# A 768 KB weight load cut into ten transfers of 64 to 3 rows, in a decode kernel with a full DMA queue

## The chip, the cores and the metric

The kernel runs on one core of one Trainium2 chip. A core has a matrix engine (PE, with PEld for its weight loads), a vector engine (DVE), a scalar engine (ACT), a general one (POOL), a queue engine (SP), and 16 DMA engines that move data between the chip's memory and the core's own memory of 128 partitions. The metric is device time in microseconds of one execution, the median over several runs. Before the change it is 1329.57 us (three runs, 1329.53 to 1329.71).

## The reference

Two blocks read the same input `x` (2 batches, 1 position, 1024 wide) and are mixed by a gate. Cut to what matters:

```python
def _A_ref(x, k_cache, v_cache, wq, wo):          # 32 heads, 16384 cached positions, 128 wide
    q = (x @ wq).reshape(B, Sq, H, Dh).transpose(0, 2, 1, 3)
    scores = jnp.einsum("bhqd,bhkd->bhqk", q, k_cache) * (Dh ** -0.5)
    p = _softmax(scores, axis=-1)
    o = jnp.einsum("bhqk,bhkd->bhqd", p, v_cache)
    return o.transpose(0, 2, 1, 3).reshape(B, Sq, H * Dh) @ wo

def _B_ref(x, w1, w2, w3, w4):
    h = _gelu(_layernorm(x) @ w1)
    ...                                            # four quarters of h shifted by 1, -1, 2, -2 positions
    x1 = x + hs @ w2
    return x1 + _gelu(_layernorm(x1) @ w3) @ w4

g = _sigmoid((x * gate_w).sum(-1, keepdims=True))
return g * a + (1 - g) * b
```

Everything is bfloat16. The two caches are 2 x 32 x 16384 x 128 each, 268 MB each, and are read once. With one position per batch, every shift moves `h` out of the sequence, so `hs` is zero; the kernel still computes `h`.

## The kernel before

All bulk data goes through one on-chip array, `mem`, of 128 partitions and five cells of 32 KB per partition. A K or V load is two heads of one batch: 8 MB, 64 KB in each partition, two cells. K of batch 0 lies in cells 0 and 1, K of batch 1 in cells 1 and 2, V in cells 3 and 4. There are 32 such units (16 head pairs by 2 batches), each with a K load (`load_k`, line 113) and a V load (`load_v`, line 118). All of them are issued by SP, in the order of the program, each as soon as the cells that it fills have been read.

For a unit, DVE transposes K in blocks (line 435), PE forms the scores (line 441), ACT the exponentials (line 479), and PE the product with V (line 495). A loop (line 684) runs over the head pairs; the last unit stands apart and issues the tail loads (`load_tail`, line 567): wo, w4 in three pieces, and the last five row groups of w1 in three pieces, each with a semaphore of its own on which PE waits. When the last piece of w1 has landed, PE adds its product (line 402), ACT applies the gelu (line 663) and the program ends; the output has been stored meanwhile (line 586).

Ahead of all this stands the start. A weight matrix of 1024 rows is laid out with eight row groups in each partition. SP issues, in this order: the first three row groups of w1 (`w1_early`, line 98: 128 partitions of 6 KB, into cell 1), the two rows of x (line 101), the row of the gate weights (line 102), and wq, 8 MB (line 91, into cells 3 and 4). ACT issues w2, 2 MB, on its own queue. PE turns x (line 235), DVE, PE and POOL compute the layer norm (`layernorm_T`), and PE multiplies the result by the three early row groups (`rows4`, line 207); ACT saves the sum in `h_early` (line 327), from which the tail goes on. Then come w2's products and wq's. The first K load goes into cells 0 and 1, over `w1_early`, and so waits on SP until PE has read it; w3 waits for wq's cells, and so on.

`in_order` (line 668) fixes the order of the instructions on each engine as the program has them.

Of the kernel before, what the change touches and what calls it, by code (L numbers as in the profile page):

```python
# [23 lines left out]
def kernel(  # L24
# [15 lines left out]
    nc = tc.nc  # L40
    P = nc.NUM_PARTITIONS
    B, Sq, D = A_x.shape
# [4 lines left out]
    KC = D // P  # L47
    FC = F // P
# [10 lines left out]
    Q4 = 4  # L59
    QP = P // Q4  # L60
    CELL = NJ * Dh // 2
    G1 = D // Q4
# [17 lines left out]
    def region(cell, elements, offset=0):  # L80
        at = cell * CELL + offset
        return mem[:, at : at + elements]

    def load_weight(W, cell, offset=0, pieces=None, queue=nc.sync):
        K, N = W.shape
        dst = region(cell, K // P * N, offset)
        src = W.rearrange("(p r) n -> p (r n)", p=P)
        r = 0
        for n in pieces or (K // P,):
            at = slice(r * N, (r + n) * N)  # L90
            queue.dma_start(out=dst[:, at], in_=src[:, at])
            r += n
        return dst.rearrange("p (r n) -> p r n", n=N)

    W1_EARLY = 3
    w1_rows = B_w1.rearrange("(p r) n -> p (r n)", p=P)
    w1_early = region(1, W1_EARLY * D)
    nc.sync.dma_start(out=w1_early, in_=w1_rows[:, 0 : W1_EARLY * D])
    w2 = load_weight(B_w2, 2, queue=nc.scalar)
    rows = const.tile([B + 1, D], BF16, name="rows")  # L100
    nc.sync.dma_start(out=rows[0:B], in_=A_x.rearrange("b s n -> (b s) n"))
    nc.sync.dma_start(out=rows[B : B + 1], in_=gate_w.unsqueeze(0))
    wq = load_weight(A_wq, 3)

    K_CELL = (0, 1)
# [11 lines left out]
    def load_v(hp, b, cell=V_CELL):  # L117
# [7 lines left out]
        out=ident_s[:], in0=ident_f[:], scalar1=-scale, scalar2=None, op0=ALU.mult  # L125
# [10 lines left out]
        out=mask4[:], in_=mask4[:], compare_op=ALU.is_ge, fill=0.0,  # L136
# [3 lines left out]
        out=mask4[:], in_=mask4[:], compare_op=ALU.is_ge, fill=0.0,  # L140
# [11 lines left out]
        out=lmat[:].rearrange("p (g h k) -> p g h k", h=2, k=4),  # L152
        in_=hm2[:].unsqueeze(1).unsqueeze(3).to_broadcast([P, P // 8, 2, 4]),
# [5 lines left out]
        out=lane[:],  # L159
        in_=ident_f[:].rearrange("p (c k) -> p k c", k=QP),  # L160
# [5 lines left out]
    for g in range(Q4):  # L166
        nc.vector.tensor_scalar(
            out=spread[:, g],
# [4 lines left out]
    oacc = [ops.tile([P, 4 * Dh], FP32, name=f"oacc{k}") for k in range(2)]  # L173
# [3 lines left out]
    arows = [ops.tile([P, G1], FP32, name=f"arow{k}") for k in range(2)]  # L177
# [18 lines left out]
    def rows4(acc, actT, weight, R, at, n, G, added=None):  # L196
        for g in range(Q4 if added is not None else 0):
            nc.tensor.matmul(
                acc[QP * g : QP * g + B, 0:n],
                lhsT=ident_b[0:B, 0:B],  # L200
                rhs=added[:, g * G + at : g * G + at + n],
                start=True,
                stop=False,
            )
        for r in range(R):
            for g in range(Q4):
                nc.tensor.matmul(
                    acc[QP * g : QP * g + B, 0:n],
                    lhsT=actT[:, r, :],
                    rhs=weight[:, r, g * G + at : g * G + at + n],  # L210
                    start=(r == 0 and added is None),
                    stop=(r == R - 1),
                )

    def turned(wide, C):
        t = mlp.tile([P, C, QP], FP32, tag="turn", name="turn")
        nc.vector.transpose(  # L217
            out=t[:].rearrange("p c k -> p (c k)"), in_=wide.rearrange("p c k -> p (c k)")
        )
        return t[:, :, 0:B]  # L220
# [13 lines left out]
    for r in range(KC):  # L234
        nc.tensor.matmul(
            rows_ps[:, r], lhsT=rows[:].rearrange("b (p r) -> b r p", r=KC)[:, r],
            rhs=ident_b[:], start=True, stop=True,
# [73 lines left out]
    xn1T = mlp.tile([P, KC, B], BF16)  # L311
    shT = mlp.tile([P, KC, B], BF16)
    xn2T = mlp.tile([P, KC, B], BF16)
    h2T = mlp.tile([P, FC, B], BF16)

    def spread_batch(t, C):
# [3 lines left out]
    compute_gate()  # L320
    layernorm_T(xT, xn1T[:], "ln1")
    nc.vector.memset(shT[:], 0.0)
    rows4(
        oacc[0], xn1T, w1_early.rearrange("p (r n) -> p r n", n=D), W1_EARLY, 0, G1, G1
    )
    h_early = const.tile([P, G1], FP32, name="h_early")
    nc.scalar.activation(out=h_early[:], in_=oacc[0][:, 0:G1], func=ACTF.Copy)
    for shift in (1, -1, 2, -2):
# [10 lines left out]
        out=x1_rows[:], in_=oacc[1][:, 0:G1], func=ACTF.Copy, scale=omg_row[:, 0:1]  # L339
# [21 lines left out]
    for k in range(2):  # L361
        wide = mlp.tile([P, 16, QP], FP32, tag="wide", name="wide")
        nc.scalar.activation(  # L363
            out=wide[:].rearrange("p (c e) i -> p c e i", e=2),
            in_=oacc[k][:].rearrange("p (c i e) -> p c e i", i=QP, e=2),
# [6 lines left out]
    for g in range(Q4):  # L372
        nc.tensor.matmul(
            qdps[:, :, :, g, :],
            lhsT=spread[:, g].rearrange("p a k -> p (a k)"),
            rhs=qb[:].rearrange("p a k x b v -> p a k (x b v)"),
            start=True,
            stop=True,
        )
    qdu = const.tile([P, NU, NV], BF16, name="qdu")  # L380
    for e in range(2):
        half = slice(e * HALF, (e + 1) * HALF)
        nc.vector.tensor_copy(
            out=qdu[half].rearrange("p u v -> p (u v)"),
            in_=qdps[half, e].rearrange("p k g n -> p (k g n)"),
# [8 lines left out]
            op=ALU.mult,  # L394
        )


    def add_rows(into, actT, first, weight, last, group):
        n = weight.shape[1] // D
        for r in range(n):  # L400
            for g in range(Q4):
                mm = nc.tensor.matmul(  # L402
                    into[g][QP * g : QP * g + B, 0:G1],
                    lhsT=actT[:, first + r, :],
                    rhs=weight[:, r * D + g * G1 : r * D + (g + 1) * G1],
                    start=False,
                    stop=(last and r == n - 1),
                    skip_group_check=True,
                )
                tc.declare_no_dep(mm.ins, group=group, reason="tail semaphores")  # L410
        return mm

    def begin_rows(into, saved):
        for g in range(Q4):
            nc.tensor.matmul(
                into[g][QP * g : QP * g + B, 0:G1],
                lhsT=ident_f[:, QP * g : QP * g + B],
                rhs=saved[:],
                start=True,
                stop=False,  # L420
                skip_group_check=True,
            )
# [103 lines left out]
    def turn_heads():  # L526
        apart = mlp.tile([P, B, H, Q4], BF16, name="apart")
        for b in range(B):
            nc.vector.tensor_tensor(
                out=apart[:, b],  # L530
                in0=o_all[:, b].unsqueeze(2).to_broadcast([P, H, Q4]),
                in1=mask4[:].unsqueeze(1).to_broadcast([P, H, Q4]),
                op=ALU.mult,
            )
        ps = misc_psum([P, B, QP])
        for b in range(B):
            nc.tensor.matmul(
                ps[:, b], lhsT=apart[:, b].rearrange("p h c -> p (h c)"), rhs=lane_b[:],
                start=True, stop=True,
            )  # L540
        t = mlp.tile([P, QP, B], BF16, name="o_turned")
        nc.vector.tensor_copy(out=t[:], in_=ps[:].rearrange("p b r -> p r b"))
        return t
# [17 lines left out]
    def tail_piece(k):  # L561
        group, cell, at, src, r, n = TAIL[k]
        return region(cell, n * D, at * D)
# [14 lines left out]
    def write_out():  # L578
        for g in range(Q4):
            at = out_row[:, g * G1 : (g + 1) * G1]  # L580
            row = arows[g][QP * g : QP * g + B, :]
            if g % 2 == 0:
                nc.vector.tensor_copy(out=at, in_=row)  # L583
            else:
                nc.scalar.activation(out=at, in_=row, func=ACTF.Copy)
        dma = nc.scalar.dma_start(out=out.rearrange("b s n -> (b s) n"), in_=out_row[:])
        dma.then_inc(stored, 16)
        tc.no_tile_sem_insts.add(dma.ins.name)
        tc.add_to_no_dep_group("stored", dma.ins)
# [53 lines left out]
    def output():  # L643
        begin_rows(arows, x1_rows)
        o_turned = turn_heads()
        hidden = [oacc[0]] * Q4
        begin_rows(hidden, h_early)
        nc.scalar.activation(
            out=h_rows[0:1, 0:1], in_=o_turned[0:1, 0, 0:1], func=ACTF.Gelu_apprx_tanh
        )  # L650
        for k, (group, cell, at, src, r, n) in enumerate(TAIL):
            nc.tensor.wait_ge(tail_sems[k], 16)
            if src is wo_rows:
                add_rows(arows, o_turned, 0, tail_piece(k), False, group)
            elif src is w4_rows:
                mm = add_rows(arows, h2T, r, tail_piece(k), r + n == FC, group)
                if r + n == FC:
                    tc.declare_fence(mm.ins, group=group)
                    write_out()
            else:  # L660
                mm = add_rows(hidden, xn1T, r, tail_piece(k), r + n == KC, group)
                tc.declare_fence(mm.ins, group=group)
        nc.scalar.activation(out=h_rows[:], in_=oacc[0][:, 0:G1], func=ACTF.Gelu_apprx_tanh)  # L663
        mark = nc.gpsimd.memset(end_mark[:], 0.0)
        tc.declare_fence(mark.ins, group="stored")
        nc.gpsimd.wait_ge(stored, 16)
# [62 lines left out]
```

## Time and profile before

| what | before |
|---|---|
| median of three runs | 1329.57 us |
| the profiled execution: time, span | 1329.7 us, 1327.7 us |
| PE busy, share of the span | 760.3 us, 57% |
| DVE busy | 647.6 us, 49% |
| ACT busy | 132.5 us, 10% |
| DMA: bytes, mean rate | 572.69 MB, 431 GB/s |
| `w1_early`: issue to landing | 8.8 us |

The profile shows one execution. The span runs from the first to the last instruction on the core; the execution's own time is longer by what lies around it. The page cuts the span into 40 slices, with a digit for the busy tenths of each engine, and for the DMA engines the mean share of the 16 and the rate. The DMA queue that SP issues to is q1, that of ACT is q10; q8 and q14 bring instructions. A transfer counts its completion on a semaphore, one step for each DMA engine that took part; the trace holds the time of each step, and start, length and size of every DMA packet.

### The profile page before, as it was taken

To read this page: it belongs to the slowest core of one execution; us is meant where nothing else is said; L and a number is where in the kernel's file an instruction comes from. 1 tells how busy PE (TensorE), PEld (TensorE's weight loads), DVE (VectorE), ACT (ScalarE), POOL (GpSimd) and SP (SyncE) were. 2 spreads that over 40 slices of the span, in tenths; PEclk is the share of its full clock that TensorE was granted. 3 is DMA by queue.
4 is the path that set the end of the run, shared out by engine and by line. 5 is a ranking of instruction groups with operands and counts; after the bars stand their busy time and mean duration, and the time that the engine had idled before them with its cause. 6 is when DMAs were issued, how large, how long until landed. Compare 5 with 4: busy or idle time off the path is not lost.

```text
span 1327.7 us, 12974 instructions
## 1 busy us (share of the span) xinstructions
PE 760.3 (57%) x4956; PEld 330.6 (25%) x4956; DVE 647.6 (49%) x507; ACT 132.5 (10%) x207; POOL 12.1 (1%) x48
## 2 busy tenths in 40 slices
PE   3465566655556665555666555566655556665554
PEld 1122222222222222222222222222222223222222
DVE  2554455554445555444555544455554445555420
ACT  0011110011111001111100111110011111101110
POOL 1000000000000000000000000000000000000000
PEclk9677888777788877778887777888777788877776
DMA  9999999999999999999999999999999999999998
GB/s 403 441 439 423 435 434 438 424 432 440 438 426 432 440 423 434 438 440 424 432 440 434 428 434 438 424 434 438 440 424 432 440 424 432 438 440 424 432 440 369
DMA packets 10820, 572.69 MB, mean 431 GB/s; under 512 B 1205, under 2 KB 1205, under 8 KB 1850
## 3 DMA queue, kind: packets, MB, share of 16 engines
q1 hardware_dynamic: 10662, 570.44, 99.4%
q10 hardware_dynamic: 148, 2.10, 0.4%
q8 instruction: 8, 0.13, 0.0%
q14 instruction: 2, 0.02, 0.0%
HBM read 572.53 MB, written 0.00 MB: 431 GB/s over the span
## 4 chain that ended last, share of the span: by engine, by line
DMA 61%; PE 11%; DVE 10%; issue 4%; ACT 0%; DVEq 0%; PEld 0%; SPq 0%; ACTq 0%
DMA mem<-in_A_k_cache_dram 59%; PE S L441 11%; DVE KT L435 10%; DMA mem<-in_B_w_dram 3%; PE oacc L495 0%; DVEq L435 0%; ACT pt L479 0%; PEld L495 0%; SPq L113 0%; PE misc L513 0%; PE oacc L402 0%; ACT osb L508 0%; PEld misc L488 0%; ACT h_rows L663 0%; PE misc L472 0%
## 5 line engine op out<-in xcount | busy, mean ns | idle before, releaser
L441 PE MATMUL S<-KT,qw 128*128 128x512 bf16 x2048 | 548.2, 418 | 363.2 <-DVE KT L435 362.8
L435 DVE STREAM_TRANSPOSE KT<-mem 128x2048 f32<-128x2048 f32 x256 | 570.7, 2282 | 270.9 <-DMA mem<-in_A_k_cache_dram 212.0
L441 PEld LDWEIGHTS <-qw 128*128 128x128 bf16 x2048 | 216.5, 106 | 686.8 <-issue 482.6
L495 PE MATMUL oacc<-mem,pt 128*8 128x512 bf16 x2048 | 118.2, 384 | 7.6 <-DMA mem<-in_A_v_cache_dram 7.6
L466 ACT ACTIVATE Dm<-ident_s,m 128x128 f32<-128x128 f32 x32 | 12.9, 402 | 978.5 <-PE oacc L495 941.4
L479 ACT ACTIVATE pt<-St,nb 64x256 bf16<-64x256 f32 x64 | 89.7, 1401 | 61.1 <-DVE nb L477 60.2
L517 DVE TENSOR_SCALAR o_all<-misc,g_rep 128x2 f32 (+1 forms) x32 | 7.0, 220 | 163.2 <-PE misc L513 163.2
L488 PE MATMUL misc<-rs,lmat 128*128 128x1 f32 x64 | 18.7, 362 | 107.9 <-ACT pt L479 61.3
L495 PEld LDWEIGHTS <-pt 128*8 128x8 bf16 x2048 | 47.3, 87 | 75.6 <-issue 23.8
L513 PE MATMUL misc<-lane,osb 128*128 128x2 f32 x256 | 33.4, 252 | 45.3 <-ACT osb L508 45.3
L489 DVE RECIPROCAL rinv<-misc 128x1 f32<-128x1 f32 x32 | 5.4, 169 | 108.5 <-PE misc L488 60.5
L462 DVE STREAM_TRANSPOSE St<-S 128x512 f32<-128x512 f32 x32 | 22.9, 717 | 66.4 <-PE L495 64.4
L513 PEld LDWEIGHTS misc<-lane,osb 128*128 128x128 f32 x256 | 31.1, 191 | 61.0 <-ACT osb L508 31.6
L488 PEld LDWEIGHTS misc<-rs,lmat 128*128 128x128 f32 x64 | 16.0, 311 | 114.8 <-ACT pt L479 65.3
L508 ACT ACTIVATE osb<-oacc,rinv 128x512 f32<-128x512 f32 x32 | 22.0, 687 | 88.3 <-PE oacc L495 88.3
L479 ACT ACTIVATION_READ_ACCUMULATOR pt<-St,nb 64x1 f32 x64 | 30.6, 477 | 0.0
L389 POOL TENSOR_TENSOR qw<-qdu,mask 128x16 bf16<-128x16 bf16 x32 | 7.3, 261 | 1161.6 <-PEq L688 1074.6
L477 DVE TENSOR_REDUCE nb<-misc 64x1 f32<-64x64 f32 x64 | 14.2, 222 | 7.0 <-PE misc L472 4.9
L472 PE MATMUL misc<-Dm,ones_f 128*128 128x128 f32 x64 | 16.6, 346 | 0.0
L464 DVE TENSOR_REDUCE m<-St 128x1 f32<-128x256 f32 x32 | 13.4, 420 | 1.1
L583 DVE CAST out_row<-arow 2x256 bf16<-2x256 f32 x1 | 0.4, 413 | 26.9 <-PE S L402 26.9
L217 DVE STREAM_TRANSPOSE turn<-wide 128x512 f32<-128x512 f32 (+2 forms) x4 | 3.0, 744 | 17.5 <-ACT wide L363 11.5
(104 smaller groups left out, 95.4 us busy)
## 6 DMA issues: line engine op xcount, KB each, us to landing
mem<-in_B_w_dram SPq DMA_DIRECT2D x1, 7168.0 KB, 31.6
mem<-in_B_w_dram SPq DMA_DIRECT2D x1, 4096.0 KB, 42.1
mem<-in_B_w_dram SPq DMA_DIRECT2D x1, 2304.0 KB, 32.2
mem<-in_B_w_dram ACTq DMA_DIRECT2D x1, 2048.0 KB, 11.8
mem<-in_B_w_dram SPq DMA_DIRECT2D x2, 768.0 KB, 21.1
mem<-in_B_w_dram SPq DMA_DIRECT2D x2, 512.0 KB, 33.9
mem<-in_A_k_cache_dram SPq DMA_DIRECT2D x32, 27.8
mem<-in_A_v_cache_dram SPq DMA_DIRECT2D x32, 32.4
```

The costliest lines, as they stand in the source:

```text
L435: nc.vector.transpose(out=kt[:], in_=Kc.rearrange("p j d -> p (j d)").bitcast(FP32))
L441: nc.tensor.matmul(S, lhsT=qw[b][:, v, NG - 1 - m : NG - 1 - m + P], rhs=ktb[:, half * GT : (half + 1) * GT, w, :, e], start=(first and n ...
L462: nc.vector.transpose(out=st[:].rearrange("p j r -> p (j r)"), in_=S[:])
L464: nc.vector.tensor_reduce(out=m[:], in_=st[:, :, 0:NG], axis=AX.XY, op=ALU.max)
L466: nc.scalar.activation(out=Dm[:], in_=ident_s[:], func=ACTF.Copy, scale=m[:, 0:1])
L472: nc.tensor.matmul(R_ps[:], lhsT=ones_f[:], rhs=Dm[:], start=True, stop=True)
L477: nc.vector.tensor_reduce(out=nb[rows], in_=R_ps[rows, rows], axis=AX.X, op=ALU.min)
L479: nc.scalar.activation(out=pts[b][rows, :, e, :].rearrange("p (m a) k -> p a k m", a=GT // 4), in_=st[rows, :, 0:NG].rearrange("p (a k) m ...
L488: nc.tensor.matmul(tot_ps[:], lhsT=lmat[:], rhs=rs[:], start=True, stop=True)
L495: nc.tensor.matmul(oacc[b][QP * q : QP * q + 8, :], lhsT=pts[b][:, g].rearrange("p h k -> p (h k)"), rhs=V[:, 4 * g : 4 * g + 4, :].rearra ...
L508: nc.scalar.activation(out=osb[:], in_=oacc[b][:], func=ACTF.Copy, scale=rinvs[b][:, 0:1])
L513: nc.tensor.matmul(ot[:], lhsT=osb[:, k * Dh : (k + 1) * Dh], rhs=lane[:, k : k + 5 : 4], start=(k == 0), stop=(k == 3),)
```

## The change

The load of `w1_early` becomes ten transfers: the first 64 partitions in the old place, ahead of x and the gate weights, and 16, 16, 10, 5, 5, 3, 3, 3 and 3 partitions behind these two and ahead of wq. All ten go through SP and count on one semaphore of their own, `early`, taken out of the framework's own bookkeeping. PE waits for all ten (160 steps) ahead of the first matmul that reads them. The matmuls are the same twelve, now recorded by `add_rows`, which moves up in the file and takes a `begin` argument.

```diff
-    nc.sync.dma_start(out=w1_early, in_=w1_rows[:, 0 : W1_EARLY * D])
+    EARLY_ROWS = (64, 16, 16, 10, 5, 5, 3, 3, 3, 3)
+    assert sum(EARLY_ROWS) == P
+    early_sem = tc.alloc_semaphore("early")
+
+    def load_early(pieces):
+        for end, n in pieces:
+            at = slice(end - n, end)
+            dma = nc.sync.dma_start(out=w1_early[at], in_=w1_rows[at, 0 : W1_EARLY * D])
+            dma.then_inc(early_sem, 16)
+            tc.no_tile_sem_insts.add(dma.ins.name)
+            tc.add_to_no_dep_group("early", dma.ins)
+
+    early_pieces = [(P - sum(EARLY_ROWS[:k]), n) for k, n in enumerate(EARLY_ROWS)]
+    load_early(early_pieces[:1])
     w2 = load_weight(B_w2, 2, queue=nc.scalar)
     rows = const.tile([B + 1, D], BF16, name="rows")
     nc.sync.dma_start(out=rows[0:B], in_=A_x.rearrange("b s n -> (b s) n"))
     nc.sync.dma_start(out=rows[B : B + 1], in_=gate_w.unsqueeze(0))
+    load_early(early_pieces[1:])
     wq = load_weight(A_wq, 3)
...
-    rows4(
-        oacc[0], xn1T, w1_early.rearrange("p (r n) -> p r n", n=D), W1_EARLY, 0, G1, G1
-    )
+    nc.tensor.wait_ge(early_sem, 16 * len(EARLY_ROWS))
+    mm = add_rows([oacc[0]] * Q4, xn1T, 0, w1_early, True, True, "early")
+    tc.declare_fence(mm.ins, group="early")
...
-    def add_rows(into, actT, first, weight, last, group):
+    def add_rows(into, actT, first, weight, begin, last, group):
...
-                    start=False,
+                    start=(begin and r == 0),
```

The slices are taken from the end: the 64 rows are partitions 64 to 127, and the last piece is partitions 0 to 2.

More of the change, by code (lines that the diff above doesn't have):

```diff
@@ L213, in rows4 @@
                 )
+    def add_rows(into, actT, first, weight, begin, last, group):
+        n = weight.shape[1] // D
+        for r in range(n):
+            for g in range(Q4):
+                mm = nc.tensor.matmul(
+                    into[g][QP * g : QP * g + B, 0:G1],
+                    lhsT=actT[:, first + r, :],
+                    rhs=weight[:, r * D + g * G1 : r * D + (g + 1) * G1],
+                    start=(begin and r == 0),
+                    stop=(last and r == n - 1),
+                    skip_group_check=True,
+                )
+                tc.declare_no_dep(mm.ins, group=group, reason="tail semaphores")
+        return mm
     def turned(wide, C):
@@ L395, in write_qw @@
         )
-    def add_rows(into, actT, first, weight, last, group):
[L399 to L405, printed above, removed]
-                    start=False,
[L407 to L411, printed above, removed]
     def begin_rows(into, saved):
@@ L653, in output @@
             if src is wo_rows:
-                add_rows(arows, o_turned, 0, tail_piece(k), False, group)
+                add_rows(arows, o_turned, 0, tail_piece(k), False, False, group)
             elif src is w4_rows:
-                mm = add_rows(arows, h2T, r, tail_piece(k), r + n == FC, group)
+                mm = add_rows(arows, h2T, r, tail_piece(k), False, r + n == FC, group)
                 if r + n == FC:
@@ L660, in output @@
             else:
-                mm = add_rows(hidden, xn1T, r, tail_piece(k), r + n == KC, group)
+                mm = add_rows(hidden, xn1T, r, tail_piece(k), False, r + n == KC, group)
                 tc.declare_fence(mm.ins, group=group)
```

## The prediction

> **What bounds the kernel now.** I read the page's slices and queues first, then the timeline of the start and the end, the windows of the end, and last the packet records of the trace.
>
> The page: slices of the DMA share, of the rate, and the queues.
> ```profile
> DMA  9999999999999999999999999999999999999998
> GB/s 403 441 439 423 435 434 438 424 432 440 438 426 432 440 423 434 438 440 424 432 440 434 428 434 438 424 434 438 440 424 432 440 424 432 438 440 424 432 440 369
> ...
> q1 hardware_dynamic: 10662, 570.44, 99.4%
> q10 hardware_dynamic: 148, 2.10, 0.4%
> q8 instruction: 8, 0.13, 0.0%
> q14 instruction: 2, 0.02, 0.0%
> ```
> The 16 DMA engines are busy from end to end, while PE, the busiest compute engine, has 57%. So only three things can move the end: more bytes (there are none: 128 rows of 6 KB before and after), a hole in the stream, or another split of the bytes over the 16 engines.
>
> Holes: the timeline of the start (start, length, engine, line).
> ```profile
> 0.80 0.38 SPq L98 DMA_DIRECT2D mem<-in_B_w_dram  x1
> 0.80 0.42 ACTq L91 DMA_DIRECT2D mem<-in_B_w_dram  x1
> ...
> 1.25 0.33 SPq L101 DMA_DIRECT2D rows<-in_A_x_dram  x1
> ...
> 1.63 0.22 SPq L102 DMA_DIRECT2D rows<-in_gate_w_dram  x1
> ...
> 1.89 0.36 SPq L91 DMA_DIRECT2D mem<-in_A_wq_dram  x1
> ...
> 17.32 0.35 SPq L113 DMA_DIRECT2D mem<-in_A_k_cache_dram  x1
> ```
> The load that waits for the changed matmuls is the first K load at 17.32. The transfer ahead of it, wq, lands its first sixteenth at 29.08 (semaphore events of the trace), so K is queued 11.8 us early. For every later load that lead is 3.7 us or more.
>
> Split: windows of the end (length; PE, PEld, DVE, ACT, POOL busy; clock; DMA share; GB/s), and the chain that ended last.
> ```profile
> 1320.00:1323.00 3.00, 1.71 (x40) 1.00 (x44) 0.00 (x0) 0.00 (x0) 0.00 (x0) 0.76 0.98 391
> 1323.00:1324.00 1.00, 0.73 (x12) 0.16 (x12) 0.24 (x1) 0.20 (x1) 0.00 (x0) 0.50 0.97 379
> 1324.00:1325.00 1.00, 0.60 (x8) 0.10 (x8) 0.59 (x2) 0.55 (x2) 0.00 (x0) 0.50 0.59 234
> 1325.00:1326.00 1.00, 0.57 (x8) 0.10 (x8) 0.00 (x0) 0.00 (x0) 0.00 (x0) 0.50 0.21 80
> ```
> ```profile
> 1291.11 34.28 DMA mem<-in_B_w_dram
> 1325.39 0.04 issue
> 1325.43 0.60 PE oacc L402 x8
> 1326.03 0.03 issue
> 1326.06 0.41 PE oacc L402 x3
> 1326.47 0.02 issue
> 1326.49 0.38 ACT h_rows L663
> ```
> The share falls 0.97, 0.59, 0.21: the engines run dry at different times, and the end hangs on the last of them. The last w1 transfer's sixteen completions come at 1324.23 plus 0, .06, .10, .23, .26, .51, .75, 1.05, 1.46, 1.50, 1.55, 1.62, 1.69, 1.70, 1.71 and 1.79 us, their mean 1.00.
>
> Where the 1.79 us come from: strung together by their times (a packet starts 3 or 4 ns before the last one on its engine ends), the packets give sixteen chains, each with 528 packets of 64 KB and under 0.2 us idle in all. So each engine is a queue that is never empty, and what it gets extra stays to the end. The eight 16 KB packets of q8 each hold one chain up for about 1.55 us, and the two 8 KB ones of q14 one each for about 0.9 and 0.7; no chain gets two of q8. Those are the eight late engines, and those at 1.05 and .75. The views do not number engines.
>
> **The change, part by part.**
> *Rows by engine.* The x transfer (2 rows) shows two packets, on two chains, and gate (1 row) one packet on one of the same two; so a small transfer uses as many engines as it has rows, beginning with the same ones. Then 64 rows are 4 on each engine, 16 are 1, and 10, 5 and 3 are 1 on the first 10, 5 and 3. In place of 8 rows each, engines 0 to 2 get 4+1+1+1+1+1+4 = 13, 3 and 4 get 9, 5 to 9 get 7, and 10 to 15 get 6. A row is 0.231 us (a 6 KB packet takes 234 ns and the next starts 3 ns before its end). A piece ends on each of its engines in a 4-byte packet of 9 ns, 6 net; they have 10, 6, 4 and 3 of these for 1 before. So engines 0 to 2 get 5 x 0.231 + 9 x 0.006 = +1.21 us, 3 and 4 +0.26, 5 to 9 -0.21, and 10 to 15 -0.45.
>
> [...]
>
> *What the end gains.* The first packets started in two groups, eight chains from 1.834 to 1.941 us and eight from 2.037 to 2.371; the x and gate chains (1.834 and 1.891) are in the first. Of the five q8 packets before 162 us, three can be put on a chain for certain, all in the second group; the other two tie with one. I take the second group for engines 8 to 15 and the late eight. Then the last of them moves from 1.79 to 1.34 (if it is among 10 to 15) or 1.58 (if it is 8 or 9), and engines 0 to 2, if they are of the five earliest, to 1.21 to 1.47. The new last is at 1.34 to 1.58, which is 0.21 to 0.45 us earlier. I take -0.30, about the middle.
>
> *Issue on SP.* Nine more issues stand ahead of wq. SP's rows take 0.22 to 0.38 us and stand 0.26 to 0.45 apart, so wq goes from 1.89 to between 4.2 and 5.9. From issue to first packet it was 1.03 us (0.80 to 1.834). Wq's first packets were at 9.19 to 9.80 on the sixteen chains; engines 10 to 15 will want theirs 0.45 earlier, the first at 8.7, so wq must be issued by 7.7. At 5.9 there are 1.8 us left: nothing. From below there is no gain either, as no chain has a hole. A piece that took as long as the 1.03 us to a first packet would cost: wq issued at 11.2, first packets at 12.2, and 3.5 us idle.
>
> *Order on the queue.* x comes behind 4 w1 rows in place of 8, each alternating with a 0.61 us w2 row, so about 4 x 0.84 = 3.4 us sooner; the layer norm from 10.36 to 16.46 moves with it, to about 13. The last rows of engines 0 to 2 end by about 10.2 (1.83 + 13 x 0.23 + 8 x 0.61 + some 0.5 of slow first packets), before that. K's first load then goes out near 14 in place of 17.32, into a queue that is full until 29: 0. If the pieces were late instead, PE would hold there with w2's and wq's matmuls queued behind it, and SP with the K load; 11.8 us cover that.
>
> *PE.* The same 12 matmuls (16.46 to 17.27), now behind a wait for ten transfers, all landed by then: 0. *End.* The store (issued 1324.71, landed 1325.96) follows the w4 piece that landed at 1322.88, which has the same spread (1.86) and moves with it.
>
> Sum: the profiled execution is 1329.70 (span 1327.7 and 2.0 around it), 0.13 over the median of 1329.57. 1329.70 - 0.30 = 1329.40, against the median 1329.27; I say 1329.3.
>
> **The rivals.**
> - *One of engines 0 to 2 is a middling one* (.51, .75 or 1.05, the last two held up by a q14 packet): it ends at 1.72, 1.96 or 2.26, that is -0.07, +0.17 or +0.47, up to 1330.0. For it: the packet at 67.5 us hit one of two or three chains tied in time, one of them x's. Chance 0.28.
> - *One of engines 0 to 2 is a late one*: 1.46 to 1.79 + 1.21, which is +0.88 to +1.21, 1330.5 to 1330.8. For it: gate's chain ties with the one that the packet at 111 us hit. Against it: the two groups. Chance 0.14.
> - *The small transfers cost issue or a fixed time* (slower): from 0.65 us a piece, (7.7 - 1.89) / 9, wq comes too late for the engines; from 0.95 us that is over 2.7 us, and at 1.03 us 3.5 us, 1333.1. Against it: w1, x and gate are followed by the next issue after 0.45, 0.38 and 0.26, and on the chains x, its completion, gate and wq follow each other without a hole. Chance 0.04.
> - *The rows are spread evenly after all* (all pieces on 16 engines by bytes): 0, 1329.6. Against it: x's two packets. Chance 0.03.
>
> [...]
>
> **How the numbers follow.** My forecast, 1329.3, has 0.50 (the -0.21 to -0.45 gives 1329.1 to 1329.4); the remaining 0.01 is for what I have not thought of. Levelling wholly would bring 1.79 - 1.00 = 0.8 us, so faster by 0.2% (2.66 us, about what a measurement here can tell) is out of reach: 0.005. Slower by that needs the issue rival: 0.04. Range: down to 1328.9 (-0.45 and some 0.2 between executions, as the median's runs span 1329.53 to 1329.71), up to 1330.4, which holds the middling and the even case and leaves out the late and the issue one.
>
> **What would show it.** Right: wq issued near 5 us and no hole before its packets; the first K load issued several us before 17; landings of K's first load still near 50.3; three chains with 13 w1 rows; the last w1 completions closer together than 1.79 us, the last by 0.2 to 0.45 sooner. Wrong: a spread of over 2 us with one or a few stragglers (the first two rivals), or a DMA share below 9 tenths near 8 us (the third).

## The result and the profile after

The change made the kernel slower: 1333.11 us (median of 10 runs, 1332.61 to 1334.01) against 1329.66 (10 runs of the kernel before on the same chip, 1329.53 to 1329.92). That is +3.45 us, a ratio of 1.0027 with a 95% interval of 1.0017 to 1.0036. The prediction was 1329.3, with 1328.9 to 1330.4 as its range. The profiled execution is the longest of the ten (1334.01, span 1331.5), so its span grew by 3.8 us, a little more than the median.

The page after: slices of the DMA share and of the rate, and the queues.
```profile
DMA  9999999999999999999999999999999999999998
GB/s 364 435 428 434 430 435 437 431 429 437 435 431 429 437 437 429 431 435 437 433 433 431 437 431 435 429 437 435 433 429 435 437 431 429 437 435 431 431 435 374
...
q1 hardware_dynamic: 10726, 570.44, 99.2%
q10 hardware_dynamic: 148, 2.10, 0.5%
q8 instruction: 8, 0.13, 0.0%
```
Queues and bytes are the same, with 64 more packets on q1, and the busy share is as full as before, from end to end. What differs is the first slice of the rate: 364 GB/s where it was 403. A slice is 33.3 us, so the engines moved 39 x 33.3 us = 1.3 MB less in it, which at the 434 GB/s of a typical slice is 3.0 us. (The page counts a packet whole in the slice in which it starts, and these are packets of 64 KB, so the figure is coarse.) No later slice pays it back. Busy engines that move less: the packets took longer.

The timeline of the start (start, length, engine, line; in brackets the idle time before and what ended it).
```profile
0.81 0.56 SPq L105 DMA_DIRECT2D mem<-in_B_w_dram  x1
...
1.43 0.47 SPq L114 DMA_DIRECT2D rows<-in_A_x_dram  x1
1.96 0.23 SPq L115 DMA_DIRECT2D rows<-in_gate_w_dram  x1
2.23 3.29 SPq L105 DMA_DIRECT2D mem<-in_B_w_dram  x9
5.56 0.36 SPq L91 DMA_DIRECT2D mem<-in_A_wq_dram  x1
...
12.17 0.57 PEld L264 LDWEIGHTS <-rows 3*128 3x128 bf16 x8 [12.17 <-DMA rows<-in_A_x_dram]
...
18.26 0.81 PE L233 MATMUL oacc<-mem,xn1T 128*2 128x256 bf16 x12 [1.26 <-DVE shT L351]
...
19.12 0.35 SPq L127 DMA_DIRECT2D mem<-in_A_k_cache_dram  x1
```
The nine issues take 3.29 us, and wq goes out at 5.56. But x, which was to come sooner, lets PE start at 12.17 in place of 10.36, and the first K load goes out at 19.12 in place of 17.32.

The windows of the end (columns as before: length; busy PE, PEld, DVE, ACT, POOL; clock; DMA share; GB/s) and the chain that ended last.
```profile
1324.00:1327.00 3.00, 1.68 (x44) 1.00 (x48) 0.00 (x0) 0.00 (x0) 0.00 (x0) 0.77 1.02 406
1327.00:1328.00 1.00, 0.54 (x16) 0.05 (x8) 0.45 (x2) 0.42 (x2) 0.00 (x0) 0.50 0.87 348
1328.00:1329.00 1.00, 0.55 (x8) 0.05 (x8) 0.38 (x1) 0.33 (x1) 0.00 (x0) 0.50 0.55 211
1329.00:1330.00 1.00, 0.77 (x12) 0.19 (x12) 0.00 (x0) 0.00 (x0) 0.00 (x0) 0.50 0.04 12
```
```profile
1294.94 34.20 DMA mem<-in_B_w_dram
1329.14 0.04 issue
1329.19 0.60 PE oacc L233 x8
1329.79 0.04 issue
1329.82 0.41 PE oacc L233 x4
1330.23 0.02 issue
1330.26 0.38 ACT h_rows L677
```
The end has the same form as before, moved as a whole: the last w1 transfer but one, with which this chain goes on to PE, is done at 1329.14 in place of 1325.39, 3.75 us later, and the last one at 1329.78 in place of 1326.02; behind them stand the same matmuls and the same gelu. The last one's sixteen completions lie 2.16 us apart where they lay 1.79; their mean is at 1328.94 in place of 1325.23 (+3.71).

When did the 3.7 us arise? The eighth and last wq packet of the sixteen engines ends on average at 32.58, before at 28.95: +3.63. So nearly all of it is there by then, and the 1297 us behind it add 0.1 at most. The packet records of the start, by what they load, mean duration of a packet before and after:

| packets | before | after | extra per engine |
|---|---|---|---|
| early w1, 6 KB, 128 | 0.309 us | 0.396 us | 0.70 us |
| w2, 16 KB, 128 | 0.633 us | 0.845 us | 1.69 us |
| first wq packet of each engine, 64 KB, 16 | 2.49 us | 3.62 us | 1.13 us |

(Extra per engine: difference of the means by 8, 8 and 1 packets.) They sum to 3.52 us, against the 3.63 to be explained. The second wq packets are plain again (2.42 before, 2.43 after). So the loss is not on w1 alone: it is also on w2, which the change doesn't touch and which comes by another queue, and on wq. How much of w2's 1.69 us the pieces of w1 cause can't be read from the means. The first packets of the start were w1's before the change, where the first 32 took 0.471 us on average (0.234 plain), and are w2's in it: the 74 w2 packets that start ahead of the first w1 row take 0.788 us on average, and in e7 below, which has no loss, 76 of them take 0.813. What tells are the 41 that start behind 6.2 us, beside w1's rows: 0.988 us on average, against 0.612 before and 0.611 in e7. Counted from e7, the excess of the change is 1.24 us on w1's rows, 0.91 on w2's and 1.13 on the first wq packets.

### The profile page after: what moved, and what is told of

It is laid out like the page before. It is cut to its first block, busy times and chain, and to the rows that moved or that the text cites. A ratio compares the mean times of both kernels' runs of the same rounds, so it can differ in the third digit from the quotient of the medians.

```text
span 1331.5 us, 12982 instructions
## 1 busy us (share of the span) xinstructions
PE 759.4 (57%) x4956; PEld 329.7 (25%) x4956; DVE 648.5 (49%) x507; ACT 132.5 (10%) x207; POOL 12.0 (1%) x48
## 4 chain that ended last, share of the span: by engine, by line
DMA 61%; PE 11%; DVE 10%; issue 4%; PEld 0%; DVEq 0%; SPq 0%; ACT 0%; PEldq 0%; ACTq 0%
DMA mem<-in_A_k_cache_dram 56%; PE S L455 10%; DVE KT L449 10%; DMA mem<-in_B_w_dram 3%; DMA mem<-in_A_v_cache_dram 2%; PE oacc L509 1%; PEld L455 0%; DVEq L449 0%; SPq L127 0%; PE oacc L233 0%; PEld misc L527 0%; ACT osb L522 0%; PEld misc L502 0%; PEldq L698 0%; ACT h_rows L677 0%
```

## The experiments

The theories in short. *Places*: a transfer that covers only a band of neighbouring partitions is slow, and slows what runs beside it. *Number*: each small transfer costs something of its own, in issue or on the engines. *Split*: the engines with more rows end later. All diffs are against the changed kernel; every run has its own runs of the kernel before, on the same chip. The table collects, for the loads of the start, the time over the plain duration (0.234 us for a 6 KB packet, 0.611 for 16 KB, 2.42 for 64 KB) summed over all engines and divided by 16, and the rate of the page's first slice.

| kernel | us | to before | ratio, 95% interval | w1 | w2 | first wq | first slice |
|---|---|---|---|---|---|---|---|
| before | 1329.66 | | | 0.60 | 0.18 | 0.07 | 403 |
| the change | 1333.11 | +3.45 | 1.0027 (1.0017 to 1.0036) | 1.30 | 1.87 | 1.20 | 364 |
| e1_halves_rows | 1332.69 | +2.87 | 1.0022 (1.0013 to 1.0032) | 1.00 | 1.77 | 0.70 | 371 |
| e2_halves_cols | 1330.07 | +0.25 | 1.0002 (0.9993 to 1.0011) | - | 0.39 | 0.00 | 403 |
| e3_dummies | 1330.20 | +0.38 | 1.0002 (0.9993 to 1.0011) | 0.57 | 0.17 | 0.16 | 404 |
| e4_act9 | 1338.72 | +8.90 | 1.0067 (1.0053 to 1.0080) | 0.82 | 1.89 | 0.78 | 336 |
| e5_eights_near | 1333.59 | +3.80 | 1.0029 (1.0017 to 1.0040) | 0.83 | 1.79 | 1.01 | 378 |
| e6_eights_apart | 1332.27 | +2.48 | 1.0018 (1.0009 to 1.0027) | 0.72 | 2.02 | 0.18 | 386 |
| e7_halves_mixed | 1329.85 | +0.06 | 1.0001 (0.9992 to 1.0010) | 0.06 | 0.96 | 0.07 | 403 |
| e8_balanced | 1332.78 | +2.99 | 1.0023 (1.0013 to 1.0033) | 1.11 | 1.96 | 0.62 | 371 |
| e9_ten_spread | 1331.25 | +1.40 | 1.0011 (1.0002 to 1.0020) | 0.15 | 0.86 | 0.74 | 397 |
| e10_ten_narrow | 1331.24 | +1.39 | 1.0011 (1.0002 to 1.0020) | 0.29 | 0.92 | 0.58 | 399 |
| e11_eights_level | 1331.20 | +1.35 | 1.0011 (1.0002 to 1.0020) | 0.21 | 0.94 | 0.54 | 403 |
| e12_halves_src | 1333.11 | +3.26 | 1.0024 (1.0014 to 1.0034) | 1.06 | 2.00 | 0.62 | 371 |

(e2's w1 packets are of 3 KB and have no plain row to be set against.)

### Number, or the way of cutting: two halves, two ways, and nine loads that nobody reads

Two transfers of 64 neighbouring partitions, which is 8 rows on each engine as before, and wq issued at 2.75:
```diff
-    EARLY_ROWS = (64, 16, 16, 10, 5, 5, 3, 3, 3, 3)
+    EARLY_ROWS = (64, 64)
```


> Edit: the early w1 rows come as two transfers of 64 rows (partitions 64 to 127 ahead of x, 0 to 63 behind the gate weights), 8 rows for each DMA engine in all, so the split over engines is the old one. Three theories of the 3.45 us. Partitions: a transfer that does not span all 128 partitions makes DMA engines write where other engines write too, and packets slow down (in the changed kernel w1's and w2's packets took 0.7 and 1.7 us per engine over their plain 234 and 611 ns). Issue: every further transfer costs serial work that makes wq's data late (first wq packets 1.1 us per engine over 2.42). Split: 13 rows on three engines. Partitions expects most of the w1 and w2 excess again, +1.2 to +2.5 us, 1330.9 to 1332.2. Issue expects a tenth of it for one more transfer, +0.1 to +0.4, at most 1330.1. Split expects 1329.6.

Two transfers of all 128 partitions, 3 KB of each:
```diff
+    EARLY_ROWS = (64, 64)
...
+            at = slice(0, half) if end == P else slice(half, 2 * half)
+            dma = nc.sync.dma_start(out=w1_early[:, at], in_=w1_rows[:, at])
```


> Edit: as the kernel with two transfers of 64 rows, but the cut goes across the row: two transfers of all 128 partitions, 3 KB each, in the same two places. Partitions expects no slow packets (a 3 KB packet near 120 ns, w2's near 611) and the old time, 1329.4 to 1329.9. Issue expects the same as for the two halves by rows, +0.1 to +0.4. Split expects 1329.6. What tells is the difference to the halves by rows: partitions says over 1 us, the other two say 0.

The whole w1 piece as before, and nine transfers of 16 to 3 rows of 512 bytes ahead of wq, into a spare tile; the numbers in it are not used:
```diff
+    for n in (16, 16, 10, 5, 5, 3, 3, 3, 3):
+        at = slice(end - n, end)
+        dma = nc.sync.dma_start(out=spare[at], in_=w1_rows[at, 0:256])
```


> Edit: w1's three row groups in one transfer again, and behind the gate weights nine further transfers of 16, 16, 10, 5, 5, 3, 3, 3 and 3 rows of 512 bytes each into a spare array that nobody reads; PE waits for them as well. So there are as many transfers as in the changed kernel, of the same row counts in the same place, with 1/12 of the bytes, and w1 in the old split. Issue expects wq's data late as in the changed kernel, first wq packets about 1.1 us over, +1.0 to +1.6 us, 1330.6 to 1331.2. Partitions expects 0 to +0.3 (few bytes on shared places). Split expects 0 to +0.1.

Two halves by rows cost 2.87 of the 3.45 us (expected were 1.2 to 2.5), with one more transfer in place of nine and an even split. Two halves by columns and the nine loads are within what can be told from nothing. The timeline of e3's start shows that the nine were issued as the pieces are:
```profile
1.91 3.15 SPq L121 DMA_DIRECT2D spare<-in_B_w_dram  x9
...
5.10 0.36 SPq L91 DMA_DIRECT2D mem<-in_A_wq_dram  x1
```
So neither the number of transfers, nor wq's issue at 5.1, is the cause; what had been expected of issue there, 1.0 to 1.6 us, did not come. The page's rate for e1 and, for contrast, e7 (below):
```profile
GB/s 371 440 436 426 434 432 437 428 437 432 437 430 435 432 437 430 435 432 437 430 435 432 437 430 435 432 437 430 435 432 437 430 435 432 437 430 435 432 437 370
```
```profile
GB/s 403 441 437 419 435 438 440 424 432 440 432 426 438 438 424 434 438 438 426 432 440 426 432 438 438 424 434 438 436 428 432 440 424 432 440 438 424 434 438 369
```
e1's first slice has 371 GB/s, e7's 403, as before.

### Which partitions, and whose addresses

The same two halves, one of all even and one of all odd partitions:
```diff
+    EARLY_ROWS = (64, 64)
...
-            at = slice(end - n, end)
+            at = slice(0 if end == P else 1, P, 2)
```


> Edit: two transfers of 64 rows as in the halves by rows, but the first takes the even partitions and the second the odd ones. [...]

The halves as in e1 where they are written, but read from w1's even and odd rows; the early product is then formed with w1's rows in another order:
```diff
+    EARLY_ROWS = (64, 64)
...
+            src = slice(0 if end == P else 1, P, 2)
+            dma = nc.sync.dma_start(out=w1_early[at], in_=w1_rows[src, 0 : W1_EARLY * D])
```


> Edit: two transfers of 64 rows into the upper and the lower half of the partitions, as in the halves by rows, but read from the even and the odd rows of w1 as in the mixed halves. The early product is so formed with w1's rows in another order; its amount of work is the same. If the places written set the time, it is that of the halves by rows, 1332.3 to 1333.2; if the places read do, that of the mixed halves, 1329.7 to 1330.1.

These two and e1 have the same number of transfers, rows, bytes and engines, and differ in the addresses alone. Written to even and odd partitions the halves cost 0.06 us; written to contiguous halves 2.87; read from even and odd rows but written to contiguous halves 3.26. (Expected for e7 were 1329.9 to 1331.2 if it matters which partitions a half holds, and 1332.0 to 1333.3 if only that it holds 64.) So the places written set it here, and the rows that are read don't. In e7 a w1 packet takes 0.241 us on average (e1: 0.359), and the first wq packets are at 2.49, as before.

Of e1's 2.87 us, by the table and counted from e7, w1's own packets carry 1.00 - 0.06 = 0.94, w2's 0.81 and the first wq packets 0.63. Why a packet takes longer that writes to a contiguous half isn't shown: no trace here tells to which partitions an engine writes, or by what way. And two transfers to disjoint halves of the partitions are not dear as such: e7's pair costs 0.06 us.

### Narrow pieces: eight neighbouring rows, or eight rows apart

The upper 64 partitions as in the change, then eight transfers of eight rows: neighbours (e5), or four partitions apart (e6).
```diff
+    EARLY_ROWS = (64, 8, 8, 8, 8, 8, 8, 8, 8)
...
+            k = 8 - end // 8
+            at = slice(HALF, P) if end == P else slice(8 * k, 8 * k + 8)
```


> Edit: 64 rows (partitions 64 to 127) ahead of x as in the change, then the other 64 as eight transfers of 8 neighbouring rows (partitions 0 to 7, 8 to 15 and so on). By the change's own counting each runs on 8 engines, so engines 0 to 7 carry 12 rows and 8 to 15 carry 4; that split alone would move the end by -0.5 to +0.25 us. Partitions (several engines writing to a few neighbouring partitions at once hold each other up) expects the first half's slowness of the two halves by rows and as much again from the eights, +2.5 to +4 us, 1332.3 to 1333.8. A theory that only the count of rows below 128 matters, and not which ones, expects the same time here and for the eights that lie apart.

```diff
+            at = slice(HALF, P) if end == P else slice(32 * (k // 4) + k % 4, 32 * (k // 4) + k % 4 + 29, 4)
```


> [...] Count, rows, bytes and engines are those of the eights that lie near. Partitions expects the packets of these eights at their plain 234 ns and the first wq packets near 2.42 us, so at least 0.8 us less than with the near ones: 1331.0 to 1332.3. Row count expects no difference (under 0.3 us) between the two.

The rows of e6 are partitions 0, 4, ..., 28, then 1, 5, ..., 29, and so on. Neighbours cost 1.32 us more than the same rows apart (1333.59 and 1332.27, and the ranges don't meet; the two profiled executions are 0.86 apart, and their packets in the table 0.71). The difference is where it should be: the first wq packets, which run beside the small pieces, are 1.01 us over plain in e5 and 0.18 in e6, while w2's excess, which in both is the slow start and the contiguous 64 rows, is nearly alike (1.79 and 2.02). And that although e6's stepped pieces let wq go out only at 8.29, where e5 has 5.12. So the narrow pieces have a share of their own in the loss, on top of the half's.

### The change's own row counts, spread over the partitions

The ten transfers with the same rows on the same engines, the first on the even partitions, the others in steps of 8 and 4 (e9), or as neighbouring odd partitions (e10):
```diff
+    PLACES = ((0, 2), (1, 8), (5, 8), (3, 4), (43, 4), (63, 4), (83, 4), (95, 4), (107, 4), (119, 4))
...
+            first, step = PLACES[k]
+            at = slice(first, first + (n - 1) * step + 1, step)
```


> Edit: the changed kernel's ten transfers with the same row counts, places in the queue and rows for each engine (13, 9, 7, 6), but with partitions that lie apart: the 64 rows are the even partitions, the two of 16 go in steps of 8, the others in steps of 4. Partitions expects the 3.45 us gone but for 0.3 at most, and then the split over engines shows alone: by the prediction's terms -0.45 to +0.47, so 1329.2 to 1330.4. If the split or the number of transfers carries part of the 3.45, it stays above 1331.

```diff
+    PLACES = ((0, 2), (97, 2), (65, 2), (45, 2), (35, 2), (25, 2), (19, 2), (13, 2), (7, 2), (1, 2))
```


> Edit: as the ten spread transfers (first the 64 even partitions), but the nine small ones take neighbouring odd partitions, so that each reaches only a narrow band. What it lies over the spread ones is the nine small transfers' share of the 3.45 us, which the first wq packets' excess (1.13 us per engine in the changed kernel, 0.7 with the two halves by rows) puts at 0.6 to 1.5 us: 1330.0 to 1331.8. If the first 64 rows alone carry all, it equals the spread ones within 0.3.

e9 takes 2.05 of the 3.45 us away. What is left has in part another cause: the strided issues are slow here (0.72 us each on average, against 0.37 in the change). The timeline of e9's start:
```profile
2.25 6.49 SPq L107 DMA_DIRECT2D mem<-in_B_w_dram  x9
8.78 0.42 SPq L91 DMA_DIRECT2D mem<-in_A_wq_dram  x1
```
Nine issues take 6.49 us in place of 3.29, so wq goes out at 8.78, later than the 7.7 that the prediction set as the limit, and the engines are idle for some 0.4 us on average ahead of wq. The rest lies on packets, above all the first wq packets (0.74 over plain). That is the prediction's issue rival, seen here, and not in the change. e10 has the same flaw (wq issued at 9.12) and the same time, so it can't tell what the narrow pieces alone cost; that it equals e9 is no evidence that they cost nothing.

### What the split is worth

Contiguous again, but even (8 rows on each engine), with five transfers:
```diff
+    EARLY_ROWS = (64, 16, 16, 16, 16)
```


> Edit: 64, 16, 16, 16 and 16 rows in place of the ten transfers: every engine carries 8 rows as before the change, in transfers of neighbouring partitions. Partitions expects the slowness of the changed kernel with the last stragglers gone: +2.5 to +3.6 us, 1332.3 to 1333.4, with the last completions no wider apart than 1.8 us. If the 13 rows on three engines carry a part of the 3.45 us, it shows as the difference, at most 1 us.

It has 1332.78 (1332.62 to 1333.99) against the change's 1333.11 (1332.61 to 1334.01): the uneven split and five more transfers are worth 0.33 us by the medians, and the ranges overlap. The spread of the last completions is 1.76, as before the change.

Spread places and a milder split (10 rows on engines 0 to 7, 6 on the others), wq issued at 6.27:
```diff
+    EARLY_ROWS = (64, 16, 16, 8, 8, 8, 8)
+    PLACES = ((0, 2), (1, 8), (5, 8), (3, 4), (35, 4), (67, 4), (99, 4))
```


> Edit: spread transfers of 64, 16, 16, 8, 8, 8 and 8 rows, by which engines 0 to 7 carry 10 rows and 8 to 15 carry 6. If the eight late engines are 8 to 15, the last completion moves from 1.79 us to the larger of 1.79 - 0.45 and 1.05 + 0.49, so 0.2 to 0.4 us sooner: 1329.3 to 1329.7, and the sixteen last completions lie within 1.6 us. If the late ones are not those, up to 0.5 us later: 1330.3, and they lie over 1.9 us apart. A version that beats the kernel before could be of this kind.

No gain: 1331.20, though wq goes out in time, so the late issue was not all of what was left in e9; the first wq packets are still 0.54 over plain, and two engines are late at the end (completions at 2.27 and 2.33 us after the first; the spread before is 1.79).

Then three kernels that put the small pieces on ACT's queue, ahead of w2, to get them out of wq's way: e9's pieces (e13), 64 and four of 16 (e14), e11's pieces (e15).
```diff
+    load_early(early_pieces[1:], nc.scalar)
     w2 = load_weight(B_w2, 2, queue=nc.scalar)
...
-    load_early(early_pieces[1:])
```


> Edit: the ten spread transfers (13, 9, 7 and 6 rows), but ACT issues the nine small ones, ahead of w2, and SP issues wq at once behind the gate weights, so that wq cannot be late for the row issues; w2 comes later, beside wq. If the 1.4 us that the ten spread transfers kept over the kernel before are late wq, this one falls to the split alone: 1329.2 to 1330.4. If it stays at 1331 or more while the one with 8 rows for each engine falls, the split costs it.

> Edit: the same arrangement with spread transfers of 64, 16, 16, 16 and 16 rows, 8 rows for each engine: the control for the split. Late wq as the cause of the 1.4 us expects 1329.6 to 1330.2, as for the mixed halves. The prediction's term says 0.3 us more than the ten ahead; the first rivals say 0.1 to 0.5 (up to 1.2) us less.

> Edit: the same arrangement with spread transfers of 64, 16, 16, 8, 8, 8 and 8 rows, 10 rows for engines 0 to 7 and 6 for 8 to 15. If engines 8 to 15 are the late ones, 0.2 to 0.4 us under the control; if the late ones are spread over all sixteen, 0.3 to 0.5 us over it.

They gave 1333.26, 1338.71 and 1333.15 (ratios 1.0027, 1.0068 and 1.0025; intervals 1.0017 to 1.0037, 1.0054 to 1.0081 and 1.0015 to 1.0035), and tell nothing of the split: the order opens faults of its own. ACT needs 7.13 us for e13's nine strided issues, so w2 goes out at 7.97 in place of 0.80; its packets then run beside wq's (11.9 to 32.7 us, in e14 18.3 to 41.1), its products come late, and the first K load is issued at 28.83 in e13.

Last, room by engine: the w1 piece whole as before, and one extra transfer of data that nothing uses, sized to delay some engines: 3 rows of 30 KB (e16, +1.16 us on engines 0 to 2), 8 rows of 18 KB (e17, +0.70 us on eight engines), 16 rows of 18 KB (e18, +0.70 us on all). The diff is e16's; e17 has `slice(0, 29, 4)`, e18 `slice(0, 121, 8)`, and both 9216 in place of 15360.
```diff
+    EARLY_ROWS = (128,)
...
+    at = slice(0, 9, 4)
+    dma = nc.sync.dma_start(out=region(0, 15360)[at], in_=spare_rows[at, 0:15360])
```


> Edit: w1's three row groups in one transfer as before the change; behind the gate weights one further transfer of 3 rows of 30 KB (w3's data, partitions 0, 4 and 8 of a cell that nobody reads until the first K load). It puts on three engines what the change's five more rows put there, 30 KB or 1.16 us, and takes nothing from the others. If engines 0 to 2 are of the five earliest (0 to 0.26 before the latest at 1.79), the end does not move: 1329.6 to 1330.0. If one of them is a middling one, up to +0.5: 1330.3. If one is a late one, +0.9 to +1.2: 1330.7 to 1331.0.

> Edit: the same with 8 rows of 18 KB (partitions 0, 4, ..., 28): 0.70 us more on eight engines. If the eight late engines are the other ones, these eight end at most at 1.05 + 0.70 = 1.75 and the end does not move: 1329.6 to 1330.0. If late ones are among them: +0.5 to +0.7, 1330.3 to 1330.6.

> Edit: the same with 16 rows of 18 KB (partitions 0, 8, ..., 120): 0.70 us more on all sixteen engines, the control. Every engine being a queue that is never empty, the whole comes at the end: +0.5 to +0.9, 1330.3 to 1330.7.

| kernel | us (range) | before | ratio, 95% interval | spread of the last completions |
|---|---|---|---|---|
| e16_more_three | 1329.85 (1329.62 to 1329.92) | 1329.77 | 1.0000 (0.9991 to 1.0009) | 1.78 |
| e17_more_eight | 1330.43 (1330.20 to 1330.53) | 1329.77 | 1.0005 (0.9996 to 1.0014) | 2.14 |
| e18_more_sixteen | 1331.42 (1331.05 to 1332.36) | 1329.77 | 1.0013 (1.0004 to 1.0022) | - |

The extra packets took 1.14 to 1.35 us in e16, which cost nothing that can be told, so engines 0 to 2 have about that much room. In e17 they took 0.68 to 0.82 us (0.74 on average) and cost 0.66, which the interval doesn't part from nothing, but the ranges don't meet: the last engine, or one within some 0.1 us of it, is among those eight. As 0 to 2 are out, that leaves 3 to 7, if an eight-row transfer runs on the first eight. e18 was to be the plain control with +0.70 and cost 1.65: its 18 KB packets took 0.765 to 1.30 us (0.687 at the rate of a plain 16 KB one, 0.611 x 18 / 16) and the first wq packets were 0.38 over plain. So rows eight partitions apart were slow here too, and the control was not free of the effect under study; nor need e9 and e11 be, whose 16-row pieces lie in such steps (first wq packets 0.74 and 0.54 over plain).

### The pieces on the other queue

The nine small pieces behind w2 on ACT's queue, so that wq goes out at 2.23:
```diff
-    load_early(early_pieces[1:])
+    load_early(early_pieces[1:], nc.scalar)
```


> Edit: the changed kernel with its nine small w1 transfers issued by ACT, behind w2, in place of SP; on SP wq follows the gate weights at once. The rows for each DMA engine are those of the changed kernel. Issue expects wq's first packets near 2.45 us again, so at least the 1.1 us of them gone: 1331.0 to 1332.0. Partitions expects w1's and w2's packets to stay slow, and the first wq packets with them, since they now run beside the small ones: 1332.3 to 1333.5. Split expects what the changed kernel has, 1333.1.

None of the theories had this: +8.90 us. The timeline of e4:
```profile
1.23 3.66 ACTq L105 DMA_DIRECT2D mem<-in_B_w_dram  x9
...
2.23 0.36 SPq L91 DMA_DIRECT2D mem<-in_A_wq_dram  x1
...
35.23 0.81 PE L233 MATMUL oacc<-mem,xn1T 128*2 128x256 bf16 x12 [17.94 <-DMA mem<-in_B_w_dram]
...
36.08 0.35 SPq L127 DMA_DIRECT2D mem<-in_A_k_cache_dram  x1
```
The pieces are issued by 4.89, but PE waits until 35.23 for the last of them, and K's first load goes out at 36.08. The packets show why: in e4 the engines take the two queues' packets in turn, so a 6 KB row (0.234 us plain), and then the 4-byte packet of its completion, each stand behind a 64 KB packet of wq (2.42 us plain), and the pieces, one behind the other, last until 34.33. Wq's last packets end at 32.39 to 33.50 and K's first start at 37.06 to 38.32: from 28 us on an engine is idle for 4.3 us on average. On top come the 2.64 us that the table gives for the slow packets of the start, and 1.5 us on later wq packets (the third ones, for one, take 2.60 to 3.30 us), together some 8.4 of the 8.90. The lead of 11.8 us that the prediction counted on is a lead only while the early pieces come ahead of wq.

## Why the prediction was wrong

The step that failed stands at its very beginning: "only three things can move the end: more bytes [...], a hole in the stream, or another split of the bytes". There is a fourth, the time that a byte takes. It went into the sum as "A row is 0.231 us" and "a 0.61 us w2 row": durations of packets of transfers over all 128 partitions, used for transfers over a contiguous half and narrower bands. Measured in the change, w1's rows took 0.396 us on average (0.241 in e7), the w2 rows beside them 0.99, and the first wq packets 3.62 in place of 2.42. The longer packets of the start are nearly the whole slip (3.52 of 3.63 us per engine), and the term was missing, not mis-sized: no row of the kernel before shows a transfer over part of the partitions but x and gate (3 rows). The prediction bounded the issue of the pieces, which that trace doesn't show either, from both sides; the duration of a row in a 64-partition transfer needed the same.

- *Rows by engine*: right as far as it shows. The trace has 64 more of the 4-byte packets than before (115 and 51 up to the end of wq), which is one for each row of the nine pieces; pieces spread over all engines would have left 9 x 16 = 144. Which engines they are isn't told.
- *What the end gains, -0.30*: not seen. The guess that the late eight are engines 8 to 15 fell with e17. With the last engine among 3 to 7 the split would be worth between +0.26 (3 or 4) and -0.21 (5 to 7) by the prediction's own terms, and not -0.30. e8's difference of 0.33 points to the former, within overlapping ranges; the split alone, with no slow packets beside it, was not seen in any run.
- *Engines 0 to 2 among the middling or late ones* (the first two rivals): fell with e16, +0.08 for +1.16.
- *Issue on SP*: right. wq was issued at 5.56, between 4.2 and 5.9 and before 7.7, and e3 shows that such an issue costs nothing that can be told. The third rival's 1333.1 is the time that came, but by another way: in the change there is no hole ahead of wq. Only e9 and e10 show it.
- *Order on the queue*: wrong. x's packets come at 10.08 to 10.27, before at 9.26 to 9.50, where I had them 3.4 us sooner, and the first K load at 19.12, not 14. In the change w2's packets come first (1.84), and the first w1 packet starts at 5.44 (before 1.83); e7, which has that too (5.49), loses nothing by it. K's lead, 32.20 (wq's first landing) less 19.12, is still 13.1 us, so the cover that the prediction named held.
- *PE and the end, 0*: right. PE's product is 0.81 us as before, and the chain's last pieces are the same.
- *What would show it*: the sign "spread of over 2 us" did come (2.16), but as a sign of the first two rivals it was misread: of the kernels with eight rows on each engine e12 has 2.09, e1 1.79 and e8 1.76.

What stays open: how the set of partitions comes to set a packet's time; why w2's packets beside w1's rows (0.99 us, before 0.612) and the first wq packets (3.62, before 2.49) are slow too, whose transfers the change leaves as they were; the split's own worth; and why the runs of the change spread over 1.4 us where those of before spread over 0.4.

## What to carry to other kernels

In these runs a packet's duration depends on the set of partitions that its transfer writes, and not on its size alone: before a transfer over all partitions is cut, take the new pieces' price from a run, and count the price for what runs beside them, which here was some three fifths of the loss (0.91 and 1.13 us, against 1.24 on w1's own rows). If a load must be cut by rows, even and odd partitions (+0.06 us) were as good as one transfer here, lower and upper half were not (+2.87); a cut by columns cost +0.25. That a piece reaches across the whole array is not enough: sixteen rows eight partitions apart were slow too (e18: 18 KB packets of 0.765 to 1.30 us, 0.687 at the plain rate).

The queue here is never empty, and the 3.63 us lost by the end of wq are still lost at the end (3.75). The busy share, 9 tenths or more in every slice but the last before and after, doesn't show them. The first slice's rate shows a large loss (364 in place of 403) and can miss a small one (e11: 403, and 1.35 us slower); the time at which the load behind the pieces ends is the surer sign (wq's last packets at 32.58 in place of 28.95).

## What the hardware did that I had not expected

- A transfer over 64 neighbouring partitions slowed the packets of other transfers beside it, on another queue too: in e1 the w2 packets that start behind 6.2 us take 0.89 us on average, where even and odd partitions (e7) leave them at 0.61, and the first wq packets 3.12, where e7 has 2.49. In e4, beside a 16-row piece, the sixteen third wq packets took 2.60 to 3.30 us (3.03 on average; plain 2.42).
- The issue of a small transfer with a step between its partitions took SP longer: 6.49 / 9 = 0.72 us on average in e9, against 3.29 / 9 = 0.37 in the change, contiguous. For the halves of 64 rows it didn't: 0.49 us for e7's odd partitions, 0.48 for e1's lower half.
- The packets of two queues came by turns, whatever their size: in the kernel before, up to some 8 us, the 6 KB w1 rows (0.234 us) and the 16 KB w2 packets (0.611) alternate on nearly every chain from the third packet on; in e4 a row of 6 KB, and its completion of 4 bytes, each stand beside a packet of 64 KB (2.42).
- When the w1 load is cut by rows, its first packets start at 5.3 to 5.7 us in place of 1.83, behind some five of w2's on each engine; in e13 to e15, where w2 is issued later, they start at 2.16. Why is not known, and by e7 it costs nothing here.
